# One scaling of the first MLP's weight conversion on GpSimd instead of ScalarE, and no products on constants between the first attention steps

## The chip, the cores and the metric

One core of a Trainium2 chip runs the whole kernel. The metric is device time in microseconds (us) of one execution, as the median of several runs. Engines are called PE (TensorE), DVE (VectorE), ACT (ScalarE), POOL (GpSimd) and SP (SyncE, which issues the DMAs). TensorE's clock has two levels, 1.2 and 2.4 GHz, and the profile gives the granted share of the higher one.

## What is computed

The reference, cut to what matters; everything is float32 outside:

```python
# q, k, v: [4, 8, 576, 64]
scores = q @ k^T / 8 - slope[h] * |i - j|, kept where 0 <= i - j < 128
attn = softmax(scores) @ v                      # -> x: [2304, 512]
h = x @ w_in                                    # w_in: [512, 2048]
x = (h * clip(h + 3, 0, 6) / 6) @ w_out         # w_out: [2048, 512]
xn = x / rms(x) * rms_g
x = (silu(xn @ w_gate) * (xn @ w_val)) @ w_out2 # 512 -> 1536 -> 512
```

The weights reach the chip as 64-bit words, and the kernel turns each into a float32 and splits that into a high and a low part for PE.

## The kernel before

The 2304 tokens are 18 tiles of 128, in six blocks of three tiles. Attention is worked out for a pair of heads and one query tile at a time (class `Step`): `scores` on PE, `bias` on DVE (L366), `exp` on ACT (L381), the reciprocal of the sum on POOL (L383 adds a constant, L384 takes the power -1), `divide` on DVE (L389), `transpose` on PE (L395), `weights` on ACT (L400, a copy out of PSUM), `values` on PE (L413). When a pair of heads has its three tiles, `finish` (L322 on ACT, L323 on DVE) splits the result for the MLP. The parts of one step are spread over consecutive time slots, one or a few in each: scores, bias and exp in one slot, divide in the next, the transpose in the one after it, the values in a fourth.

The order of the work is written out by hand and each engine works through its own queue in that order. There are two parts that matter here.

*Stage A*, in the text below: the loop over `AHEAD` = 15 slots at L568, ahead of the first MLP. In each slot PE gets scores, transposes and values of three different attention steps, and then `busy(1)` (L564), a product of a constant tile with itself whose result nobody reads; PE runs it as two passes. Before the loop there are three more of these (`busy(WARM)`). In slots 4 to 11 the stages of the conversion of the weight units 0 and 1 are mixed in (L590, L591).

*Stage B*: the steps of the first MLP, a loop at L690 over 12 of the 16 chunks of the hidden layer for block 0, and then over all 16 for block 1. One step m does `product1` (L476; 12 products, x by w_in) into one PSUM bank, the attention's transposes, scores and values of this slot, relu on ACT (L714), the product h * min(r, 6) on DVE (L715, one input from PSUM), divide, a copy of the high part on ACT (L720), bias, the low part on DVE (L726), exp, and `product2` of the step before (L489; 9 products by w_out). Until the sixteen weight units are converted, each step also carries one unit (L739 to L744). After that, some 135 us into the span, the kernel goes on with the other blocks and the second MLP. Of the diff, these later parts see only a new argument in a call (L204), with which the instruction stays where it was.

The conversion of one unit, 1024 words in each of 128 partitions, is the generator `convert` (L116). Each `yield` ends one stage, and `First.step(k, stages)` runs the named stages of unit k:

- stage 0: y, the low word scaled (L128, ACT);
- stage 1: x, the high word scaled by 2^-112 (L133, ACT). It reads every other 32-bit word of the raw tile and writes a dense tile, which has two buffers;
- stage 2: the sign bit (L137, DVE);
- stage 3: x and y put together (L140, DVE, two inputs);
- stage 4: the high part for PE (L142, ACT);
- stage 5: the low part for PE (L144, DVE, two inputs).

In a step of stage B, unit k = m + 1 goes through stages 3, 4 and 5, and the unit after it through 0, 1 and 2:

```python
                if k < M1:
                    W1.step(k + 1, 0)
                    W1.step(k, 3, 4)
                    W1.step(k + 1, 1, 2)
                    W1.step(k, 5)
```

So stages 1 of fourteen units stand in stage B, and those of units 0 and 1 in stage A. POOL's queue holds, in a step of stage B with attention, L383 and L384 of that step (its exp stands ahead of the conversion). `load` (L158) brings the raw units by DMAs on SP's queue, some units ahead. The second MLP's weights go through the same generator (L204), with the low word on DVE.

Of the kernel before, what the change touches and what calls it, by code (L numbers as in the profile page):

```python
# [10 lines left out]
F32 = mybir.dt.float32  # L11
# [4 lines left out]
AF = mybir.ActivationFunctionType  # L16
ALU = mybir.AluOpType
# [7 lines left out]
DM = H * D  # L25
# [40 lines left out]
def f32(ap):  # L66
    return ap.bitcast(F32)
# [3 lines left out]
def fused_kernel(ctx: ExitStack, tc: tile.TileContext, qd, kd, v, w1, w2, rms_g, out):  # L71
# [7 lines left out]
    vec, act, pool, pe, sp = nc.vector, nc.scalar, nc.gpsimd, nc.tensor, nc.sync  # L79
# [33 lines left out]
        pool.memset(rel_split[HALF:, : P + HALF], BIG)  # L113


    def convert(raw, n, p, y_bufs, x_bufs, low_on):  # L116

        words = raw.bitcast(U32).rearrange("p (n t) -> p n t", t=2)
        low, high = words[:, :, 0], words[:, :, 1]
        y = p.tile([P, n], U32, tag="wy", name="wy", bufs=y_bufs) if y_bufs else low
        if low_on is act:
            act.activation(y, low, AF.Copy, scale=7.49 * 2.0**-32)  # L128
        else:
            vec.tensor_scalar(y, low, 29, None, ALU.logical_shift_right)  # L130
        yield
        x = p.tile([P, n], F32, tag="wx", name="wx", bufs=x_bufs)
        act.activation(x, high.bitcast(F32), AF.Copy, scale=2.0**-112)  # L133
        yield
        quarters = raw.bitcast(U16).rearrange("p (n t) -> p n t", t=4)
        halves = y.bitcast(U16).rearrange("p (n t) -> p n t", t=2) if y_bufs else quarters[:, :, :2]
        vec.tensor_scalar(halves[:, :, 1], quarters[:, :, 3], 0x8000, None, ALU.bitwise_and)  # L137
        yield
        xi = x.bitcast(U32)
        vec.scalar_tensor_tensor(out=xi, in0=xi, scalar=3, in1=y, op0=ALU.logical_shift_left, op1=ALU.bitwise_or)  # L140
        t = yield x
        act.copy(t[:, 0], x)  # L142
        yield
        vec.tensor_sub(t[:, 1], x, f32(t[:, 0]))  # L144
        yield

    def room(k, shape, dtype, name):
        return wpool.tile(shape, dtype, tag=f"w{k}", name=name)

    class First:  # L150
# [12 lines left out]
        def step(self, k, *stages):  # L163

            for i in stages if k < M1 else ():
                if i == 0:
                    self.runs.append(convert(self.raw[k], 2 * DM, cpool, 2, 2, act))
                if i == 4:
                    t = room(k, [P, 2, 2 * DM], F32R, "w")
                    self.tiles.append(t)  # L170
                    self.runs[k].send(t)
                else:
                    next(self.runs[k])
# [9 lines left out]
    class Second:  # L183
# [17 lines left out]
        def begin(self):  # L201

            if self.raw:
                self.run = convert(self.raw.pop(0), DM, wcpool, 1, 3, vec)  # L204
                for _ in range(3):
                    next(self.run)

# [63 lines left out]
    class Pair:  # L271
# [42 lines left out]
        def finish(self):  # L314

            nq = self.n * P
            x = self.acc.rearrange("p u q -> p (u q)")[:, :nq]
            if self.j == 0:
                xs = (x0pool if self.b == 0 else xpool).tile([P, KC, 2, 3 * P], F32R, tag="xs", name="xs")
                xs_of[self.b] = [xs[:, c] for c in range(KC)]  # L320
            t = xs_of[self.b][self.j]
            act.copy(t[:, 0, :nq], x)  # L322
            vec.tensor_sub(t[:, 1, :nq], x, f32(t[:, 0, :nq]))  # L323

    class Step:
# [12 lines left out]
        def scores(self):  # L338
            pr, c0, k0 = self.pair, self.c0, (self.i - 1 - self.pair.lo) * P
            for x, y in PARTS_OF if pr.parts else ():  # L340
                for a, s in enumerate(self.s):
                    rows = slice(a * D, (a + 1) * D)
                    pe.matmul(  # L343
                        s[:, c0:],
                        lhsT=pr.qs[rows, x, self.u * P : (self.u + 1) * P],
                        rhs=pr.ks[rows, y, k0 + c0 : k0 + 2 * P],
                        start=(x == 0 and y == 0),
                        stop=(x == 1),
                    )
            for a, s in enumerate(self.s if not pr.parts else ()):  # L350
                rows = slice(a * D, (a + 1) * D)
                pe.matmul(  # L352
                    s[:, c0:],
                    lhsT=pr.qr[rows, self.u * P : (self.u + 1) * P],
                    rhs=pr.kr[rows, k0 + c0 : k0 + 2 * P],
                    start=True,
                    stop=True,
                )
# [70 lines left out]
    for k, pr in enumerate(pairs):  # L429
        b, j = divmod(k, H // 2)  # L430
        if b < 2:
            t0, plan = 3 * j if b == 0 else AHEAD - 3 + 3 * j, {"S": (0, 1, 2), "D": (1, 2, 3), "T": (2, 3, 4), "V": (3, 4, 5)}
        else:
            t0, plan = AHEAD + M1 * (b - 1) - 4 + 4 * j, {"S": (0, 0, 2), "D": (1, 1, 3), "T": (None, 3, None), "L": (1, None, 3), "V": (4, 4, 4)}
        slots["Q"].setdefault(t0 - (2 if b < 2 else 1), []).append(pr)
        for u in range(pr.n):
            step = Step(pr, u)
            for kind, at in plan.items():
                if at[u] is not None:
                    slots[kind].setdefault(t0 + at[u], []).append(step)  # L440

    def at(t):
        return [slots[kind].get(t, []) for kind in KINDS]

    def prepare(pairs_, steps):

        for pr in pairs_:
            pr.split() if pr.parts else pr.scale()
        for x in steps:
            k = pairs.index(x.pair) + 2  # L450
            if x.last and k < len(pairs):
                pairs[k].load()
# [98 lines left out]
    cpool = conv.enter_context(tc.tile_pool(name="cpool", bufs=2))  # L551
# [10 lines left out]
    def busy(n):  # L562
        for _ in range(n):
            pe.matmul(warm[:, : 2 * P], lhsT=rel[:, :P], rhs=rel, start=True, stop=True)  # L564
# [3 lines left out]
    for t in range(AHEAD):  # L568
        q, s_, d_, t_, _, v_ = at(t)
        scores(s_, t % 2)  # L570
        for x in t_:
            x.transpose()
        for x in v_:
            x.values()
        busy(1)
        for x in t_:
            x.weights()
        for x in s_:
            x.bias()
        prepare(q, s_)  # L580
        for x in d_:
            x.divide()
        for x in v_:
            if x.last:
                finish(x.pair)
        for x in s_:
            x.exp()
        if t == 2:
            W1.load(3)
        W1.step(0, *{4: (0,), 5: (1, 2), 7: (3,), 9: (4, 5)}.get(t, ()))  # L590
        W1.step(1, *{8: (0,), 11: (1, 2)}.get(t, ()))  # L591
# [83 lines left out]
    for p, (b, m0, m1) in enumerate(PARTS):  # L675
        n = BLOCKS[b][1]
# [13 lines left out]
        for m in range(m0, m1):  # L690
# [3 lines left out]
            if p == 3 and m == 2:  # L694
                first.close()
                wcpool = second.enter_context(tc.tile_pool(name="wcpool", bufs=1, side="right", **OPEN))
# [40 lines left out]
            if p < 2:  # L737
                k = m + 1 if p == 0 else CUT + 1 + m
# [10 lines left out]
            if last:  # L749
# [6 lines left out]
                for x in early:  # L756
                    k = m - EARLY[x.m]
# [20 lines left out]
    n = 3 * P  # L778
# [208 lines left out]
```

## Time and profile before

| what | us |
|---|---|
| median of 3 runs | 967.47 (966.93 to 967.69) |
| the profiled execution | 966.15 |
| its span, first to last instruction | 964.4 |
| PE busy | 948.7 (98%) |
| DVE busy | 640.4 (66%) |
| ACT busy | 454.8 (47%) |
| POOL busy | 183.7 (19%) |

Times in rows are counted from the start of the span. In a row of the timeline the brackets say how long the engine was idle before the instruction and what ended that. A group's row gives the busy time of all, the mean of one in ns, and behind the bar the idle time before them. In the chain of waits each piece is the time from one release to the next, so that pieces add up to the span. A busy PE is not PE at its peak.

### The profile page before, as it was taken

How to read it: one execution, taken by the hardware profiler on the slowest of the kernel's cores; microseconds unless marked ns; L12 is line 12 of the kernel's file. 1: busy time of each engine (PE TensorE's matmuls, PEld its weight loads, DVE VectorE, ACT ScalarE, POOL GpSimd, SP SyncE). 2: the span in 40 equal slices, each digit the busy share in tenths (PEclk: the TensorE clock that was granted, in tenths of full speed). 3: DMA queues.
4: the chain of work that ended last, by engine and by line, in shares of the span. 5: the costliest groups of instructions: out<-in, count | busy, mean ns of one | idle time of the engine just before them, and what ended most of it. 6: DMA issues, size and time to landing. Idle time of an engine off the chain costs nothing.

```text
span 964.4 us, 14723 instructions
## 1 busy us (share of the span) xinstructions
PE 948.7 (98%) x5366; PEld 835.6 (87%) x5366; DVE 640.4 (66%) x1336; ACT 454.8 (47%) x969; POOL 183.7 (19%) x327
## 2 busy tenths in 40 slices
PE   8999999999999999999999999999999999999998
PEld 5687778888888888888999999999999999999996
DVE  5788774454788777777567657787645577545555
ACT  6899763354656655665455453433132323131120
POOL 4333012222322422332033222210000000000000
PEclk9999999999999999999999999999999999999999
DMA  7446511113466465554436757876657555755521
GB/s 230 166 162 196 225 31 31 31 50 107 158 213 200 145 190 169 171 166 135 140 130 226 265 223 278 323 277 232 229 201 275 216 215 217 262 197 205 212 96 65
DMA packets 67432, 175.02 MB, mean 181 GB/s; under 512 B 5024, under 2 KB 41888, under 8 KB 62624
## 3 DMA queue, kind: packets, MB, share of 16 engines
q1 hardware_dynamic: 67360, 174.09, 51.8%
q8 instruction: 42, 0.69, 0.3%
q14 instruction: 30, 0.25, 0.1%
HBM read 130.03 MB, written 44.04 MB: 180 GB/s over the span
## 4 chain that ended last, share of the span: by engine, by line
PE 89%; DVE 5%; ACT 3%; issue 1%; DMA 1%; POOL 0%; ACTq 0%; POOLq 0%; DVEq 0%
PE ps_o L489 19%; PE ps_h L476 19%; PE ps_y L874 15%; PE ps_o L827 10%; PE ps_S L827 8%; PE ps_A L827 6%; PE ps_h L827 4%; PE ps_av L413 3%; PE ps_t L395 2%; PE ps_s L352 2%; PE ps_s L343 1%; ACT wx L133 1%; PE warm L564 1%; DMA wraw<-w 1%; DVE wx L140 1%
## 5 line engine op out<-in xcount | busy, mean ns | idle before, releaser
L489 PE MATMUL ps_o<-w,g 128*128 128x512 f32 x864 | 223.4, 401 | 3.3 <-DVE w L144 3.0
L476 PE MATMUL ps_h<-xs,w 128*128 128x384 f32 x1152 | 223.0, 342 | 0.1
L476 PEld LDWEIGHTS ps_h<-xs,w 128*128 128x128 f32 x1152 | 202.0, 189 | 4.8 <-PE warm L564 0.5
L489 PEld LDWEIGHTS ps_o<-w,g 128*128 128x128 f32 x864 | 157.0, 188 | 43.1 <-DVE w L144 6.2
L874 PE MATMUL ps_y<-wo,g 128*128 128x512 f32 x648 | 150.2, 390 | 0.5 <-DVE g L863 0.5
L874 PEld LDWEIGHTS ps_y<-wo,g 128*128 128x128 f32 x648 | 121.4, 188 | 25.1 <-DVE g L863 0.9
L715 DVE SCALAR_TENSOR_TENSOR t<-t,ps_h 128x384 f32<-128x384 f32 x96 | 53.1, 554 | 120.3 <-ACT t L714 120.2
L714 ACT ACTIVATE t<-ps_h,three 128x384 f32<-128x384 f32 x96 | 55.7, 580 | 99.7 <-PE ps_h L476 99.7
L881 DVE TENSOR_TENSOR y<-y,ps_y 128x512 f32<-128x512 f32 x90 | 61.7, 685 | 35.0 <-PE ps_y L874 34.8
L720 ACT CAST g<-t 128x384 fp32r<-128x384 f32 x96 | 49.3, 513 | 52.2 <-DVE t L715 51.0
L381 ACT ACTIVATE t<-t,m 128x128 f32<-128x128 f32 (+1 forms) x144 | 61.1, 426 | 21.5 <-DVE t L373 10.5
L383 POOL TENSOR_SCALAR r<-den 128x2 f32<-128x2 f32 x72 | 30.1, 418 | 215.1 <-ACT t L381 214.3
L850 ACT ACTIVATE r<-r 128x384 f32<-128x384 f32 x36 | 18.9, 525 | 104.6 <-DVE r L849 104.6
L827 PE MATMUL ps_o<-S,tw 128*128 128x384 f32 x336 | 66.2, 339 | 0.3 <-DVE t L847 0.3
L726 DVE TENSOR_TENSOR g<-t,g 128x384 fp32r<-128x384 f32 x96 | 54.5, 567 | 13.9 <-ACT g L720 12.4
L827 PEld LDWEIGHTS ps_o<-S,tw 128*128 128x128 f32 x336 | 59.3, 188 | 1.4 <-DVE u L838 0.8
L384 POOL TENSOR_TENSOR r<-r,minus 128x2 f32<-128x2 f32 x72 | 55.8, 775 | 6.0
L402 POOL TENSOR_SCALAR_AFFINE_SELECT pt<-pt 128x256 f32<-128x256 f32 x82 | 36.8, 449 | 95.6 <-ACT pt L400 92.7
L835 ACT COPY s<-ps_S 128x384 f32<-128x384 f32 x18 | 8.6, 480 | 89.7 <-PE ps_S L827 89.7
L366 DVE CUSTOM_DVE_ANT_0 t<-ps_s,rel 128x256 f32<-128x256 f32 (+2 forms) x128 | 45.2, 394 | 4.2 <-PE ps_s L352 4.2
L140 DVE SCALAR_TENSOR_TENSOR wx<-wx,wy 128x512 uint32<-128x512 uint32 (+1 forms) x52 | 44.2, 849 | 0.0
L133 ACT ACTIVATE wx<-wraw 128x512 f32<-128x512 f32 (+1 forms) x52 | 42.7, 822 | 0.0
(138 smaller groups left out, 1479.3 us busy)
## 6 DMA issues: line engine op xcount, KB each, us to landing
tw<-t SPq DMA_DIRECT2D x52, 896.0 KB, 6.4
wraw<-w SPq DMA_DIRECT2D x36, 512.0 KB, 4.3
wo<-w SPq DMA_DIRECT2D x18, 1024.0 KB, 5.1
wraw<-w SPq DMA_DIRECT2D x16, 1024.0 KB, 7.9
t<-th SPq DMA_DIRECT2D x12, 896.0 KB, 4.4
t<-tl SPq DMA_DIRECT2D x12, 896.0 KB, 4.2
b<-wx SPq DMA_DIRECT2D x24, 256.0 KB, 2.5
w<-w SPq DMA_DIRECT2D x12, 512.0 KB, 2.9
```

The costliest lines, as they stand in the source:

```text
L133: act.activation(x, high.bitcast(F32), AF.Copy, scale=2.0**-112)
L140: vec.scalar_tensor_tensor(out=xi, in0=xi, scalar=3, in1=y, op0=ALU.logical_shift_left, op1=ALU.bitwise_or)
L381: act.activation(p, p, AF.Exp, bias=self.m[:, a : a + 1], scale=-1.0, accum_out=self.den[:, a : a + 1])
L384: pool.tensor_tensor(self.r, self.r, minus, ALU.pow)
L476: pe.matmul(ps[:, : n * P], lhsT=w[:, a, c * P : (c + 1) * P], rhs=xs[c][:, b, : n * P], start=(k == 0), stop=(k == 3 * KC - 1),)
L489: pe.matmul(o, lhsT=g[:, a, i * P : (i + 1) * P], rhs=w[:, b], start=(m == first and a == 0 and b == 0), stop=(m == last and a == 1),)
L714: act.activation(r[:, :nq], ps[:, :nq], AF.Relu, bias=three)
L715: vec.scalar_tensor_tensor(out=r[:, :nq], in0=r[:, :nq], scalar=6.0, in1=ps[:, :nq], op0=ALU.min, op1=ALU.mult)
L726: vec.tensor_sub(g[:, 1, :nq], r[:, :nq], f32(g[:, 0, :nq]))
L827: pe.matmul(ps, lhsT=w[a][:, k, c * P : (c + 1) * P], rhs=x[:, b, c], start=(start and j == 0), stop=(j == 5), skip_group_check=True,)
L874: pe.matmul(ps, lhsT=gs[i + k][:, a, t // 3, t % 3 * P : (t % 3 + 1) * P], rhs=wo[i + k][:, b], start=(k == 0 and a == 0 and b == 0), stop ...
L881: vec.tensor_add(acc[t], acc[t], ps)
```

## The change

The generator gets an argument that says which engine scales the high word. The first MLP's units pass `pool`, the second MLP's pass `act`, as it was. The product on constants in each of the 15 slots of stage A is left out; the three ahead of the loop stay.

```diff
-    def convert(raw, n, p, y_bufs, x_bufs, low_on):
+    def convert(raw, n, p, y_bufs, x_bufs, low_on, high_on):
...
         x = p.tile([P, n], F32, tag="wx", name="wx", bufs=x_bufs)
-        act.activation(x, high.bitcast(F32), AF.Copy, scale=2.0**-112)
+        if high_on is act:
+            act.activation(x, high.bitcast(F32), AF.Copy, scale=2.0**-112)
+        else:
+            pool.tensor_scalar(x, high.bitcast(F32), 2.0**-112, None, ALU.mult)
         yield
...
-                    self.runs.append(convert(self.raw[k], 2 * DM, cpool, 2, 2, act))
+                    self.runs.append(convert(self.raw[k], 2 * DM, cpool, 2, 2, act, pool))
...
-                self.run = convert(self.raw.pop(0), DM, wcpool, 1, 3, vec)
+                self.run = convert(self.raw.pop(0), DM, wcpool, 1, 3, vec, act)
...
         for x in v_:
             x.values()
-        busy(1)
         for x in t_:
             x.weights()
```

## Rows read from the trace of the kernel before

**Rows 1.** The chain of waits in stage A, one piece: start us, us, what
```profile
20.85 0.63 PE warm L564 x2
```

**Rows 2.** Windows, most of stage A: us, busy per engine, PEclk, DMA share, GB/s
```profile
10.00:40.00 30.00, 27.96 (x199) 16.44 (x200) 22.29 (x86) 24.84 (x73) 12.67 (x27) 1.00 0.51 164
```

**Rows 3.** Waits, 0 to 39 us: us in total, times, longest us
```profile
DVE t L366 <- PE ps_s L352: 4.2, 4, 1.8
...
DVE t L389 <- POOL r L384: 4.0, 9, 0.7
...
DVE w L144 <- ACT w L142: 1.5, 1, 1.5
```

**Rows 4.** The chain of waits in stage B, pieces of product1: start us, us
```profile
62.90 2.12 PE ps_h L476 x12
...
81.82 2.10 PE ps_h L476 x12
...
125.81 3.51 PE ps_h L476 x12
```

**Rows 5.** Groups by shape, 0 to 130 us: busy, mean ns, idle before
```profile
L133 ACT ACTIVATE wx<-wraw 128x1024 f32<-128x1024 f32 x16 | 18.5, 1154 | 0.0
...
L715 DVE SCALAR_TENSOR_TENSOR t<-t,ps_h 128x384 f32<-128x384 f32 x14 | 7.8, 554 | 6.5 <-ACT t L714 6.5
...
L726 DVE TENSOR_TENSOR g<-t,g 128x384 fp32r<-128x384 f32 x14 | 7.7, 553 | 0.7 <-ACT g L720 0.6
```

**Rows 6.** Timeline, steps of stage B: start us, us, instruction, [idle before it]
```profile
42.13 0.55 DVE L715 SCALAR_TENSOR_TENSOR t<-t,ps_h 128x384 f32<-128x384 f32 x1 [2.58 <-ACT t L714]
...
63.69 0.75 POOL L383 TENSOR_SCALAR r<-den 128x2 f32<-128x2 f32 x1 [3.83 <-ACT t L381]
...
64.52 0.95 POOL L384 TENSOR_TENSOR r<-r,minus 128x2 f32<-128x2 f32 x1
...
65.60 1.23 DVE L144 TENSOR_TENSOR w<-wx,w 128x1024 fp32r<-128x1024 f32 x1 [0.17 <-ACT w L142]
...
76.08 1.89 POOL L383 TENSOR_SCALAR r<-den 128x2 f32<-128x2 f32 x1 [3.80 <-ACT t L381]
...
78.06 0.71 POOL L384 TENSOR_TENSOR r<-r,minus 128x2 f32<-128x2 f32 x1
...
78.43 1.23 DVE L144 TENSOR_TENSOR w<-wx,w 128x1024 fp32r<-128x1024 f32 x1 [0.49 <-ACT w L142]
...
79.96 0.55 DVE L715 SCALAR_TENSOR_TENSOR t<-t,ps_h 128x384 f32<-128x384 f32 x1 [0.31 <-ACT t L714]
...
80.43 0.54 DVE L389 TENSOR_SCALAR t<-t,r 128x192 f32<-128x192 f32 x2
```

**Rows 7.** Groups by shape, GpSimd, whole span
```profile
L104 POOL TENSOR_SCALAR_AFFINE_SELECT rel<-rel 128x256 f32<-128x256 f32 x1 | 0.4, 398 | 0.1
...
masks.py:199 POOL TENSOR_SCALAR_AFFINE_SELECT ident<-ident 128x128 f32<-128x128 f32 x1 | 0.3, 293 | 0.1
```

**Rows 8.** Timeline, GpSimd in stage A
```profile
24.67 0.22 POOL L383 TENSOR_SCALAR r<-den 128x2 f32<-128x2 f32 x1 [0.83 <-ACT t L381]
```

**Rows 9.** Waits, 48 to 97 us (stage B, nearly eight steps)
```profile
PEld ps_o L489 <- DVE w L144: 2.9, 6, 0.8
...
DVE t L715 <- ACT t L714: 2.5, 8, 0.3
```

**Rows 10.** Timeline at 494 us: a GpSimd sum and a VectorE instruction
```profile
494.33 0.73 POOL L243 TENSOR_TENSOR tx<-tx 128x256 f32<-128x256 f32 x1
...
494.39 1.08 DVE L726 TENSOR_TENSOR g<-t,g 128x384 fp32r<-128x384 f32 x1 [0.58 <-ACT g L720]
```

**Rows 11.** Windows around a fall of the granted clock (columns as in rows 2)
```profile
122.90:125.20 2.30, 0.02 (x1) 0.05 (x1) 2.02 (x4) 1.68 (x3) 0.00 (x0) 1.00 0.00 0
...
126.00:129.50 3.50, 3.50 (x13) 3.06 (x14) 3.01 (x4) 2.37 (x3) 0.00 (x0) 0.51 0.02 5
```

**Rows 12.** Timeline, PE in stage A
```profile
30.43 0.43 PE L395 MATMUL ps_t<-ident,t 128*128 128x128 f32 x2 [1.27 <-DVE t L389]
```

## The prediction

> **What bounds the kernel now.** I read the page first: the matrix engine (PE) is busy 98% of the span, so only places where it waits, or works on what nobody needs, can give time back. The code that the diff touches runs in the first 135 us alone, and the chain of the work that ended last shows what sets the pace there. The reader is to see two stages.
>
> *Stage A* (5 to 39 us): fifteen attention steps before the first MLP. Nearly every step's piece of the chain holds a product on constants, 0.63 us of PE [rows 1]. It looks as if PE set the pace. The windows of this stage correct that: of 30 us VectorE (DVE) is busy 22.3 and ScalarE (ACT) 24.8 [rows 2]. The waits of the stage say who is late next: DVE waits for PE's scores 4.2 us in four waits, 1.8 of it before the first scores of all; it waits for GpSimd's (POOL's) reciprocal 4.0 us in nine, and 1.5 us once for ACT's cast of a weight unit [rows 3].
>
> *Stage B* (39 to 135 us): each step has a product1, a product2 and one weight unit. A unit goes through wy (L128), L137, wx (L133), L140, L142, L144. Three steps of the chain take 81.82 - 62.90 = 18.92 us, 6.3 a step [rows 4], and pieces of L133 stand on it. ACT spends 18.5 us on its sixteen L133 [rows 5]; that is its busy time, not what its absence is worth. In the timeline of a step, L144 on DVE waits for L142 on ACT, which waits for L140 on DVE. L133 delays none of these three. It delays L714, and DVE's next work, L715, waits 0.31 for it [rows 6]. So L133 costs 0.3 a step: L144 holds DVE until that short before L715.
>
> **Part 1, the products on constants.** Fifteen steps give up 0.63 us each, 9.5 us of PE work. Not more can come back than DVE waits for PE: 4.2 less the first 1.8, so 2.4 us [rows 3]. Not less than nothing, as long as the clock holds (below). I take **-0.8 us**, a third: DVE already waits for the reciprocal in nine steps of fifteen [rows 3], and scores that come earlier turn partly into a longer wait for that, or for ACT's cast.
>
> **Part 2, the new instruction.** POOL does what L133 did: 1024 elements a partition, one input. No such instruction is in the trace. The nearest one-input rows are affine_select, 0.29 us for 128 elements and 0.40 for 256 [rows 7]: 0.82 ns an element, so 0.398 + 768 x 0.00082 = **1.03 us**. For the lower end I put the smallest tensor_scalar, 0.22 us for two elements [rows 8], beside the 0.40 for 256: 0.7 ns an element, 0.93 us. For the upper end the 256-element time is taken four times, 1.59 us. I choose 1.03, as the two rows that differ in nothing but length are nearest.
>
> *In stage A* two are moved. ACT is freed of two, POOL's queue gets two, and the next reciprocal (L383, L384), for which DVE's L389 waits, queues behind each. If nothing hides that, it costs 2 x 1.03 = 2.1 us; if POOL has room and ACT was last at one of them, one L133 is gained, 18.5 / 16 = 1.1 us [rows 5]. Neither end is nearer to a row, so I take the middle, **+0.5 us**.
>
> *In stage B* fourteen are moved. The gain: L715's waits for L714 sum to 6.5 us in fourteen [rows 5], of which the first, 2.58 at 42.13, is the start of the stage [rows 6]. The other thirteen, 3.9 us, vanish: **-3.9 us**. PE can follow: in the stretch where these waits are gone in eight steps (2.4 us), PE waits 2.9 us for L144 [rows 9].
>
> The price: POOL and DVE keep each other out. POOL's 128x2 L383 needs 0.22 us alone [rows 8] but 1.89 while L140 and L137 run on DVE [rows 6]. It holds the other way too: L726, 0.55 us in the mean [rows 5], takes 1.08 when it starts 0.06 after a POOL sum of 0.73 [rows 10]. DVE was free to start when POOL had run 0.59 us, 0.14 before its end. So a POOL wx of 1.03 us keeps such a DVE instruction out for 0.89 us. With PSUM as one input DVE is not kept out: L383 takes 0.22 in the middle of L323 [rows 8].
>
> Now place it. On POOL it stands behind L383 and L384 of its step, both of which are themselves late. In the step at 76 us L384 ends at 78.77, L144 has begun at 78.43, so POOL begins when that ends, 79.66. L715 reads PSUM and runs at once. L389, due 0.47 after it, at 80.13, is held until 79.66 + 0.89 = 80.55, that is 0.42 late [rows 6]. Five of the nine steps with attention are like this one (L383 of 1.08 or 1.89 us). In the other four (L383 of 0.75, as at 63.69) L384 ends at 65.47 and POOL's next begins some 0.08 later, 0.05 before L144 at 65.60 [rows 6]. If POOL is first, L144 is 0.84 late, and with it product2 on PE; if L144 is first, L389 is 0.42 late again. That is too near to call, so I take the middle, 0.63. Sum: 5 x 0.42 + 4 x 0.63 = **+4.6 us** (ends 3.8 and 5.5). In the five steps without scores ahead POOL has nothing else, runs beneath L715 and the wait for L720's cast, and costs nothing; without that cover it would be 0.4 each. No DMA is issued or moved. POOL's queue is free again some 1.7 us before the next L383.
>
> The Trainium skill ("SBUF — State Buffer", section "SBUF: two separate sides") says that whichever of the two starts first has the shared pair for the whole instruction. The trace agrees that it is a hold and no sharing, but shows DVE starting 0.14 us before POOL's end; by the rule the nine steps would cost 9 x 0.14 = 1.3 us more, and the sum below would be +1.7.
>
> **Sum:** -0.8 + 0.5 - 3.9 + 4.6 = **+0.4 us** on the profiled execution's 966.15 us (span 964.4 us). The median of the runs shown is 967.47, 1.3 above it, so the forecast is 967.47 + 0.4 = **967.9 us**: no change that can be measured. A measurement of this kernel can tell about 0.2% (1.9 us) from none.
>
> **The rivals.** *Slower: POOL's instruction is long.* At 1.59 us each hold is 0.56 longer; place: L389 or L144 in nine steps, 9 x 0.56 = 5.0 us, so +5.4 and **972.9**. It decides from about 1.2 us on, where the sum passes 0.2%. For it: a two-input sum of 256 elements takes POOL 0.73 us [rows 10], so POOL is slow where it has more to do, and the input has every other word. Against it: the two one-input rows. The Trainium skill ("GPSIMD Engine Reference", section "Performance pitfalls for Q7 kernels") gives about 1.9 cycles an element for steps of up to 8 bytes; an estimate from that page is 1024 x 1.9 / 1.2 GHz = 1.6 us, and no row here shows such a step on POOL.
>
> *Faster: the hold costs nothing.* If POOL's instruction finds gaps of DVE (it waits 0.49 us for L142 and 0.31 for L714 in the step at 76 us [rows 6]) or lets DVE pass, the 4.6 falls away: -4.2, **963.3**. Against it speaks L726's 1.08; for it, that no row shows a POOL instruction as long as this one beside DVE.
>
> *The clock.* At 122.9 to 125.2 PE was idle 2.3 us, and from 126.0 to 129.5 the granted clock was 0.51, that is 1.2 instead of 2.4 GHz; product1 took 3.5 us there instead of 2.1 [rows 4, 11]. In stage A PE waits 1.27 us before 30.43 [rows 12], and the clock stays at 1.00 [rows 2]; without the 0.63 us product before that wait the gap grows to 1.9 [rows 1, 12]. If the clock falls there too, +1.4 us: **969.3**. The Trainium skill ("TensorE: Matmul & The Clock Gate", section "Part 1") says that activity is what releases the throttle, so that products on constants do work by being there; by that page stage A could lose more than once.
>
> **How the numbers follow.** Forecast 0.40, long POOL instruction 0.26, no hold 0.20, clock 0.14. The forecast's own bounds (parts 1 and 2 at their ends, -2 and +3) put 0.04 of it below and 0.02 above the 0.2%; of the clock's case 0.06 stay within. Faster: 0.20 + 0.04 = 0.24. Within: 0.34 + 0.06 = 0.40. Slower: 0.26 + 0.02 + 0.08 = 0.36. The range reaches from the case without a hold to that of the long instruction, 963.4 to 973.2; the forecast's own is 966 to 970.
>
> **What would show it.** Right: POOL's wx near 1.03 us; L715's waits for L714 gone; in their place L389 about 0.4 late behind POOL, L144 late in some steps; three steps of the chain at 18.9 to 19.3 us; a stage A shorter by half a microsecond or so; PE in stage A waiting more, at a clock of 1.00. Wrong: a wx of 1.5 us or more; no wait of L389 or L144 for POOL; a granted clock of 0.5 before 39 us; a chain that loses or gains time after 135 us, where nothing was changed.

## The result, and the profile after

The changed kernel took **974.11 us** (median of 6 runs) against 967.42 for the kernel before, run beside it: 1.0072 times as long, 95% interval [1.0061, 1.0083], so 7.0 us slower by the ratio. The forecast was 967.9 with a range up to 973.2; the result lies just above the range. Two later comparisons gave 1.0068 [1.0052, 1.0083] and 1.0058 [1.0044, 1.0071].

The page's group of the moved instruction, and the groups of VectorE in stage B (39 to 144 us), after; the columns are those of [rows 5]:

```profile
L136 POOL TENSOR_SCALAR wx<-wraw 128x1024 f32<-128x1024 f32 x16 | 52.1, 3261 | 4.1 <-DVE w L147 4.1
...
L143 DVE SCALAR_TENSOR_TENSOR wx<-wx,wy 128x1024 uint32<-128x1024 uint32 x15 | 19.1, 1276 | 1.7 <-POOL wx L136 1.7
...
L717 DVE SCALAR_TENSOR_TENSOR t<-t,ps_h 128x384 f32<-128x384 f32 x16 | 8.8, 547 | 3.6 <-ACT t L716 3.6
```

wx takes 3.26 us in the mean where the forecast had 1.03. (From L133 on, line numbers after are three higher, behind the loop of stage A two higher.) The waits of L717 (the old L715) for the relu are gone except one: 3.6 us, all of it in one wait.

Windows after, columns as in [rows 2]: four of stage A and the start of stage B, then one in the middle of stage B.

```profile
10.00:20.00 10.00, 9.28 (x56) 5.36 (x54) 6.02 (x27) 7.63 (x25) 3.51 (x8) 0.67 0.82 303
20.00:30.00 10.00, 6.41 (x44) 3.98 (x45) 7.32 (x23) 6.73 (x22) 7.19 (x10) 0.85 0.23 70
30.00:40.00 10.00, 6.82 (x58) 4.12 (x56) 8.66 (x27) 6.61 (x20) 5.70 (x7) 0.98 0.23 72
40.00:50.00 10.00, 8.65 (x46) 7.20 (x45) 4.08 (x18) 4.45 (x14) 3.02 (x7) 0.66 0.66 245
60.00:70.00 10.00, 9.93 (x59) 7.85 (x60) 9.24 (x22) 7.06 (x18) 9.77 (x5) 1.00 0.80 272
```

Two things have changed. The granted clock, 1.00 in all of stage A before [rows 2], falls three times before 50 us. And GpSimd, busy some 40% of stage A, is busy 9.77 of 10 us in the middle of stage B.

Where the time went, by the starts of TensorE's product1 in both traces: the first starts at 43.54 instead of 39.12 (+4.4 us); the third at 56.74 instead of 49.93 (+6.8); the fifteenth at 134.15 instead of 125.56 (+8.6). From 144 us on the distance is constant, +7.7; the 0.9 between is made up where the clock fell before, at 126 us [rows 11], and did not fall after. So more than half is lost in stage A, where the forecast had -0.3, and 2.4 of the rest in the first two steps of stage B.

Here is the place in stage A where the first wx runs, timeline after: start us, us, instruction, [idle before it]; then two rows of the same place in the kernel before.

```profile
19.50 0.71 POOL L387 TENSOR_TENSOR r<-r,minus 128x2 f32<-128x2 f32 x1
...
20.18 2.83 POOL L136 TENSOR_SCALAR wx<-wraw 128x1024 f32<-128x1024 f32 x1
20.25 1.43 DVE L392 TENSOR_SCALAR t<-t,r 128x256 f32<-128x256 f32 x2 [0.48 <-POOL r L387]
...
21.56 0.63 PE L398 MATMUL ps_t<-ident,t 128*128 128x128 f32 x4 [1.73 <-DVE t L392]
...
22.29 0.94 DVE L302 TENSOR_SCALAR qraw<-qraw,qscale 128x384 f32<-128x384 f32 x1
...
23.10 0.23 POOL L386 TENSOR_SCALAR r<-den 128x2 f32<-128x2 f32 x1
...
24.16 0.48 DVE L392 TENSOR_SCALAR t<-t,r 128x128 f32<-128x128 f32 x2 [0.93 <-POOL r L387]
```

```profile
19.06 0.62 DVE L389 TENSOR_SCALAR t<-t,r 128x256 f32<-128x256 f32 x2 [0.47 <-POOL r L384]
...
21.36 0.48 DVE L389 TENSOR_SCALAR t<-t,r 128x128 f32<-128x128 f32 x2
```

When the reciprocal (L387) ends, it releases two things at once: wx, next in GpSimd's queue, and VectorE's L392, which waits for that reciprocal. wx is first by 0.07 us, and L392's pair takes 1.43 us instead of 0.62. TensorE waits 1.73 us for it. That is one delay, the hold. The other is the queue: the next reciprocal (L386 at 23.10) begins when wx has ended, and the next L392 waits 0.93 us for it. That L392 comes 3.91 us after the one before it, against 2.30 in the kernel before.

The chain of waits says which delay counts here: it does not go through the held pair but through wx and the reciprocal behind it (start us, us, what):

```profile
20.21 2.81 POOL wx L136
...
23.10 0.23 POOL r L386
...
23.40 0.73 POOL r L387
...
24.16 0.30 DVE t L392
```

It does so again at the second wx, from 37.02, at both in wx_only and after_third below, and at the first in wx_only_again. In after_again it goes through the held pairs instead, and through TensorE at its lower clock behind them. So the hold is not far behind the queue.

Of the 4.4 us, 1.2 are lost before the first wx starts (20.25 against 19.06), and 3.2 from there to the first product1 (23.29 us against 20.06).

In stage B the chain of waits after runs through GpSimd (start us, us, what):

```profile
63.77 1.79 POOL r L386
...
65.64 0.72 POOL r L387
66.36 3.58 POOL wx L136
...
69.97 1.24 DVE wx L143
```

wx, then the two halves of the reciprocal behind it: 3.6 + 1.8 + 0.7 = 6.1 us of a step of 6.4. GpSimd is at its limit there. Yet the step is hardly longer: from the fifth to the eighth product1 three steps take 88.44 - 69.22 = 19.2 us after, 18.9 before [rows 4]. What stage B loses beyond its first two steps is 1.8 us up to the fifteenth product1, in a few single steps.

### The profile page after: what moved, and what is told of

Its sections match the earlier page's. It is cut to its first block, busy times and chain, and to the rows that moved or that the text cites. A ratio compares the mean times of both kernels' runs of the same rounds, so it can differ in the third digit from the quotient of the medians.

```text
span 972.3 us, 14661 instructions
## 1 busy us (share of the span) xinstructions
PE 946.0 (97%) x5336; PEld 834.7 (86%) x5336; DVE 649.3 (67%) x1336; ACT 439.1 (45%) x953; POOL 242.2 (25%) x343
## 4 chain that ended last, share of the span: by engine, by line
PE 85%; DVE 5%; POOL 5%; ACT 3%; issue 2%; ACTq 0%; POOLq 0%; DVEq 0%
PE ps_o L492 18%; PE ps_h L479 18%; PE ps_y L876 15%; PE ps_o L829 10%; PE ps_S L829 8%; PE ps_A L829 6%; PE ps_h L829 4%; PE ps_av L416 3%; POOL wx L136 3%; PE ps_t L398 2%; PE ps_s L346 1%; POOL r L386 1%; PE ps_s L355 1%; DVE w L147 1%; POOL r L387 1%
## 5 line engine op out<-in xcount | busy, mean ns | idle before, releaser
L717 DVE SCALAR_TENSOR_TENSOR t<-t,ps_h 128x384 f32<-128x384 f32 x96 | 53.1, 553 | 116.5 <-ACT t L716 116.4
L386 POOL TENSOR_SCALAR r<-den 128x2 f32<-128x2 f32 x72 | 33.1, 460 | 163.8 <-ACT t L384 162.2
L852 ACT ACTIVATE r<-r 128x384 f32<-128x384 f32 x36 | 18.9, 526 | 106.9 <-DVE r L851 106.9
L387 POOL TENSOR_TENSOR r<-r,minus 128x2 f32<-128x2 f32 x72 | 56.2, 780 | 6.0
L136 POOL TENSOR_SCALAR wx<-wraw 128x1024 f32<-128x1024 f32 x16 | 52.1, 3261 | 4.1 <-DVE w L147 4.1
L398 PE MATMUL ps_t<-ident,t 128*128 128x128 f32 x190 | 35.7, 291 | 14.4 <-DVE t L392 12.6
```

The costliest lines, as they stand in the source:

```text
L136: pool.tensor_scalar(x, high.bitcast(F32), 2.0**-112, None, ALU.mult)
L387: pool.tensor_tensor(self.r, self.r, minus, ALU.pow)
L398: pe.transpose(self.ps[:, a, c], self.t[:, a, c * P : (c + 1) * P], ident)
L717: vec.scalar_tensor_tensor(out=r[:, :nq], in0=r[:, :nq], scalar=6.0, in1=ps[:, :nq], op0=ALU.min, op1=ALU.mult)
```

## The experiments

Two theories to begin with. *POOL*: the long wx is the loss, as a hold on VectorE and as GpSimd's queue. *Clock*: without the products the granted clock falls in stage A. One more kernel, forms, was executed once (974.9 us), for its trace. All ratios are against the kernel before, run beside each on the same chip, whose median was 966.6 to 966.9; 0.1% is 1 us. "First product1" is its start in the trace, 39.12 before and 43.54 after.

| kernel | wx | products | ratio [95%] | first product1 |
|---|---|---|---|---|
| products_only | ScalarE | out | 0.9996 [0.9987, 1.0006] | 38.52 |
| wx_only | GpSimd | kept | 1.0054 [1.0041, 1.0068] | 42.30 |
| half_first | half on GpSimd, stage B | kept | 0.9984 [0.9975, 0.9993] | 38.78 |
| after_again | GpSimd | out | 1.0068 [1.0052, 1.0083] | 42.00 |
| late_units | GpSimd in stage B only | out | 1.0021 [1.0012, 1.0030] | 38.76 |
| pool_copy | GpSimd, a copy | out | 1.0030 [1.0014, 1.0047] | 41.64 |
| copy_later | the same, later in stage A | out | 1.0016 [1.0006, 1.0025] | 40.78 |
| no_wx | none | kept | 0.9972 [0.9960, 0.9984] | 38.99 |
| no_wx_no_products | none | out | 0.9953 [0.9937, 0.9970] | 39.80 |
| wx_only_again | GpSimd | kept | 1.0044 [1.0029, 1.0059] | 44.82 |
| after_third | GpSimd | out | 1.0058 [1.0044, 1.0071] | 42.73 |

### One part of the change at a time

products_only, against before:

```diff
-        busy(1)
```

> Only the products on constants are left out; ScalarE scales the high words as before. Theory 'clock' (the fall of TensorE's granted clock in stage A comes from the missing products alone and is most of the loss): granted clock 0.5 in records before 48 us, first product1 at 41 to 43.5 us instead of 39.12, program 1.5 to 4.5 us slower than before. Theory 'POOL' (the 2.83 us instruction is the loss): granted clock 1.00 in stage A, first product1 at 38.3 to 39.2, program 0 to 0.8 us faster. Theory 'both together' (the clock falls only where wx lengthens TensorE's gaps too): clock 1.00 or one short fall, within 1 us of before.

Measured: 0.9996, first product1 0.60 us earlier, still 0.61 earlier at 144 us. Windows of this kernel, columns as in [rows 2]:

```profile
10.00:20.00 10.00, 8.34 (x57) 5.02 (x58) 6.69 (x30) 8.36 (x26) 3.70 (x8) 0.83 0.81 293
20.00:30.00 10.00, 6.49 (x57) 3.80 (x55) 7.40 (x28) 8.04 (x24) 4.57 (x8) 1.00 0.31 92
30.00:40.00 10.00, 9.05 (x62) 6.04 (x63) 7.61 (x31) 8.40 (x26) 4.03 (x9) 0.83 0.30 95
```

The clock does fall, in two of three windows, and it costs nothing that shows: TensorE has room here (6.49 of 10 us busy where the clock is full). So neither theory had it whole. The missing products are enough for a fall; this fall is not the loss. What TensorE did before a fall is seen best in the changed kernel, windows of after, and then the first stretch in the kernel before:

```profile
21.00:27.40 6.40, 3.81 (x33) 2.68 (x34) 5.47 (x18) 3.61 (x12) 5.02 (x6) 0.96 0.30 93
27.50:30.90 3.40, 3.40 (x21) 1.91 (x21) 1.34 (x7) 3.21 (x8) 1.75 (x4) 0.58 0.06 15
```

```profile
21.00:27.40 6.40, 6.14 (x44) 3.40 (x44) 4.71 (x17) 5.59 (x17) 3.34 (x7) 1.00 0.35 104
```

Busy 3.81 of 6.40 us, then a clock of 0.58; before, with the products, 6.14 of 6.40 and no fall. The Trainium skill ("TensorE: Matmul & The Clock Gate", section "Part 1") says that activity is what releases the throttle, and the traces agree so far that the clock fell where TensorE had done less.

wx_only, against after:

```diff
+        busy(1)
```

> Only wx goes to GpSimd; the products on constants stay. Theory 'POOL': each wx 2.8 us in stage A and 3.6 in stage B; two of them delay stage A by 1.5 to 2.5 us (first product1 at 40.6 to 41.6); GpSimd paces the steps with scores (wx 3.6, r 1.8 and 0.7: 6.2 to 6.4 us a step), clock 1.00 before 48 us, program 3 to 5 us slower than before. Theory 'clock': first product1 before 40.3, program 0 to 1.5 us slower than before. Theory 'both together': 1.5 to 3.5 us slower, clock 1.00.

Measured: 1.0054, +5.2 us. First product1 42.30 (+3.2), at 144 us +4.7. Timeline of wx_only in stage A:

```profile
18.87 2.85 POOL L136 TENSOR_SCALAR wx<-wraw 128x1024 f32<-128x1024 f32 x1
18.93 1.45 DVE L392 TENSOR_SCALAR t<-t,r 128x256 f32<-128x256 f32 x2 [0.48 <-POOL r L387]
```

The same collision with the products kept, at a granted clock of 1.00 from 10 to 30 us. Here too the chain goes through wx and the reciprocal behind it, for 2.82 us at 18.90 and 2.83 at 35.72. That is the POOL theory, and stage A is dearer than even it had (40.6 to 41.6).

### What wx costs on GpSimd, and why

forms: the sixteen wx in four shapes in turn.

```diff
+            form = len(W1.runs) % 4 if W1.tiles else 0
...
+                    pool.tensor_scalar(x[:, c], high.bitcast(F32)[:, c], 2.0**-112, None, ALU.mult)
...
+                pool.tensor_copy(x, high.bitcast(F32))
+                pool.tensor_scalar(x, x, 2.0**-112, None, ALU.mult)
```

> As wx_only, but the sixteen wx take turns in four forms: one instruction of 1024 (as in after), four of 256, a copy of 1024 from every other word followed by a product by a number in place on dense words, two of 512. If the every-other-word input is what makes it slow: the dense product takes 0.9 to 1.6 us and the copy 2.8. If the operation is slow whatever the layout: both 2.8, 256 columns 0.7 and 512 columns 1.4. If a fixed part is large: 256 columns take over 0.9.

Timeline of forms, GpSimd in stage A, where little runs beside it:

```profile
20.23 2.85 POOL L138 TENSOR_SCALAR wx<-wraw 128x1024 f32<-128x1024 f32 x1
...
37.01 1.12 POOL L144 COPY wx<-wraw 128x1024 f32<-128x1024 f32 x1
38.21 2.79 POOL L145 TENSOR_SCALAR wx<-wx 128x1024 f32<-128x1024 f32 x1
```

It is the operation. The copy from every other word takes 1.12 us, the product on dense words 2.79, as much as on every other word. The 512-column form takes 1.54 where VectorE does not hinder it, so 2.85 - 1.54 = 1.31 us for 512 columns more: 2.6 ns an element and a fixed part of 0.2. (Four of 256 took 3.98, all of them beside VectorE's work.) The Trainium skill ("GPSIMD Engine Reference", section "Performance pitfalls for Q7 kernels") prices a read by its step, some 1.9 cycles at steps up to 8 bytes, by which an estimate was 1.6 us. That a step of 8 bytes costs no more than dense words agrees with it; that the operation changes the time 2.5 times is not in it, and the estimate fits neither.

This allows the sharpest test of the forecast: a wx of the size that it assumed. In pool_copy wx is that copy. The exponent is mended by an exclusive-or in the two VectorE instructions that follow in any case, so nothing is added.

```diff
-            pool.tensor_scalar(x, high.bitcast(F32), 2.0**-112, None, ALU.mult)
+            pool.tensor_copy(x, high.bitcast(F32))
...
+            vec.tensor_scalar(halves[:, :, 1], quarters[:, :, 3], 0x8000, 0xC000, ALU.bitwise_and, ALU.bitwise_xor)
...
+        vec.scalar_tensor_tensor(out=xi, in0=xi, scalar=3, in1=y, op0=ALU.logical_shift_left, op1=ALU.bitwise_or if high_on is act else ALU.bitwise_xor)
```

> After, with wx as a copy on GpSimd (the exponent is mended by an exclusive-or in the two VectorE instructions that follow, so nothing else is added): 1.1 us alone instead of 2.83. If the size of that one instruction was the step that failed: the forecast's sum with 1.1 for 1.03, +0.5 to +1.5 us, 967.1 to 968.1; VectorE's relu wait gone, reciprocals 0.4 late. If GpSimd's hold is not the price at this size: 3 to 4.5 us faster than before. If the clock falls in stage A even so: 1.5 to 4 us slower than before.

Measured: 1.0030, +2.9 us, against +6.6 for the changed kernel beside it. So the length of wx is worth 3.7 us (by the medians, 970.53 and 972.97, 2.4), and 2.9 us stay although wx has the forecast's size. They are not in stage B alone (the 0.5 to 1.5 us expected from the size alone are missed; the 1.5 to 4 us expected if the clock falls in stage A even so are met, and it does fall). The first product1 is at 41.64, nearly as late as in after_again (42.00). Timeline of pool_copy in stage A:

```profile
19.04 1.09 POOL L136 COPY wx<-wraw 128x1024 f32<-128x1024 f32 x1
19.13 1.43 DVE L395 TENSOR_SCALAR t<-t,r 128x256 f32<-128x256 f32 x2 [0.48 <-POOL r L390]
```

L395 (the L392 of this kernel) takes 1.43 us behind a GpSimd instruction of 1.09 just as behind one of 2.83. **The hold of a VectorE instruction that starts just behind it is 0.81 us in both, and does not grow with the length.** The Trainium skill ("SBUF — State Buffer", section "SBUF: two separate sides") lets whoever starts first have the shared pair for the whole instruction; beside the copy that fits within 0.2 us, beside the 2.83 us product it does not: VectorE gets in some 2 us before its end. A later part of the long instruction keeps out other work, though: L302 takes 0.94 at 22.29 after, 0.42 in the mean before the first MLP in products_only.

With the short copy the queue is no longer in the way: the next L395, at 21.64, waits for nothing, nor does the one at 38.48 behind the second copy. What costs time is the held pair and, behind it, TensorE's clock. Windows of pool_copy, the first with TensorE's wait of 1.73 us for that pair, the second behind it:

```profile
18.00:20.40 2.40, 0.71 (x6) 0.30 (x4) 1.92 (x7) 1.33 (x5) 2.17 (x4) 1.00 0.23 72
21.00:24.00 3.00, 3.00 (x17) 1.69 (x18) 2.87 (x9) 1.59 (x6) 1.70 (x3) 0.50 0.03 5
```

From the L395 at 19.13 the next comes only 0.2 us later than in the kernel before (2.51 us against 2.30), but the third one 1.6 us later (8.23 against 6.65). The chain between goes through TensorE at half clock, from 21.07 to 24.74.

### Is it the hold, the queue or the clock in stage A?

copy_later, against pool_copy: in stage A the copy waits until VectorE has begun its products with the reciprocal, by a one-column memset of its tile behind them.

```diff
+        W1.step(0, *{6: (2,)}.get(t, ()))
+        W1.step(1, *{12: (2,)}.get(t, ()))
...
+                vec.memset(x[:, :1], 0.0)
             pool.tensor_copy(x, high.bitcast(F32))
```

> As the kernel with wx as a copy on GpSimd, but in stage A the copy is made to wait until VectorE has begun its next product with the reciprocal (a one-column memset of the tile behind that product, on VectorE), one step later than before. Theory 'the hold' (wx starts on GpSimd at the moment at which its own reciprocal releases VectorE's product, and keeps that product out for 0.85 us, twice): the two products take 0.62 instead of 1.43, first product1 at 39.0 to 40.3 instead of 41.64, program 1 to 2.5 us faster than with the copy at its old place (968 to 969.5). Rival 'the queue' (the next reciprocal waits for wx, wherever it stands): first product1 at 41 to 42.2, no gain. Rival 'the clock': the products are short but records of 0.5 stay between 20 and 48 us, first product1 at 40.5 to 41.6.

Timeline of copy_later:

```profile
20.26 0.62 DVE L401 TENSOR_SCALAR t<-t,r 128x256 f32<-128x256 f32 x2 [0.48 <-POOL r L396]
...
20.97 1.14 POOL L143 COPY wx<-wraw 128x1024 f32<-128x1024 f32 x1 [0.74 <-DVE wx L142]
...
21.49 0.83 DVE L311 TENSOR_SCALAR qraw<-qraw,qscale 128x384 f32<-128x384 f32 x1
22.19 0.22 POOL L395 TENSOR_SCALAR r<-den 128x2 f32<-128x2 f32 x1
```

The two products with the reciprocal are back at 0.62 us, and the first product1 comes at 40.78, 0.86 us earlier than with the copy in its old place; 1.0016 against 1.0030, medians 968.60 and 970.53 (the intervals overlap). The next reciprocal (L395) still stands behind the copy, and VectorE's product with it now waits 0.92 us; the gain came in spite of that queue. It is at the low end, and the first product1 is later than the 40.3 expected: the hold has moved to L311 (0.83 instead of 0.42), and in this profile the clock had fallen before the first copy ran (0.66 from 10 to 20 us). From 20 us on it is 1.00, as it was not in pool_copy (0.83 and 0.90 in the next two windows). The first product that pool_copy holds starts 1.13 us later here, at 20.26, so from there on copy_later takes 20.52 us to its first product1 and pool_copy 22.51. These 2.0 us are the hold and the falls of the clock behind it together: both are absent in copy_later from 20 us on, so it does not tell one from the other. By its number alone, 40.78 would also lie in the rival's range (40.5 to 41.6), whose falls between 20 and 48 us are not there.

late_units, against after:

```diff
-                    self.runs.append(convert(self.raw[k], 2 * DM, cpool, 2, 2, act, pool))
+                    self.runs.append(convert(self.raw[k], 2 * DM, cpool, 2, 2, act, act if k < 2 else pool))
```

> After, with the first two units' wx back on ScalarE; the other fourteen stay on GpSimd, the products stay out. Theory 'stage A is most of it' (two wx of 2.83 us ahead of the reciprocal, and the clock that falls with them): first product1 at 38.3 to 38.8, no record of 0.5 after 41 us, stage B costs 1 to 2 us, program 0.3 to 1.5 us slower than before. Rival 'stage B is most of it' (GpSimd as the pace): 3.5 to 5.5 us slower than before although stage A is as fast as without the products.

Measured: 1.0021, first product1 38.76. Beside after_again's 1.0068 in the same comparison: the first two units, of sixteen, cost 0.47%, **4.5 of 6.6 us**; the other fourteen 2.0, or 2.4 over products_only. The theory that stage A is most of it is right, though its 0.3 to 1.5 us for the rest was too little.

### Are the products worth keeping once wx is on GpSimd?

after_again, after_third (the changed kernel unaltered) and wx_only_again:

> The changed kernel unaltered, beside the others of this group. From its first profile: granted clock 0.5 in records between 10 and 48 us, first product1 near 43.5, the constant part after 144 us +7.7. If the falls of the clock in stage A belong to this kernel, they are here again and it is 1 to 3 us slower than the kernel that moved wx and kept the products (+5.1 us); if they were chance, this profile has a clock of 1.00 and the loss is 5 to 5.5 us.

> wx on GpSimd, products kept, once more, beside the changed kernel on the same chip: what the products are worth when wx is there. If they keep the clock up for the delayed stage A: 1.2 to 3 us less than the changed kernel. If they only cost their time: 0 to 0.6 us more than it.

> The changed kernel beside the one that keeps the products: 1.2 to 3 us slower than that if the falls of the clock in stage A are a price, and its profile shows between three and six records of 0.5 before 48 us; equal or 0.6 faster if not.

The clock falls in stage A in every profile of the changed kernel. It also falls in the profiles that keep the products with wx on GpSimd, once each in stage A and later: wx_only 0.83, wx_only_again 0.73, forms 0.83 from 30 to 40 us. Windows of after_again:

```profile
10.00:20.00 10.00, 8.03 (x54) 4.75 (x54) 6.47 (x28) 7.80 (x26) 4.32 (x9) 0.83 0.79 291
20.00:30.00 10.00, 8.22 (x58) 4.91 (x58) 6.98 (x24) 6.89 (x19) 6.87 (x9) 0.83 0.23 68
30.00:40.00 10.00, 6.88 (x40) 4.24 (x42) 8.48 (x27) 5.98 (x20) 5.69 (x7) 0.71 0.23 72
```

The price as a whole stays open. Within one comparison the changed kernel is 1.0058 and the one that keeps the products 1.0044: 1.4 us apart, but the intervals overlap. Single profiles show why it is hard to tell: where a fall lies differs from one to the next. In the first profile of after, one covers the first product1 (3.89 us for eleven of its products from 43.54; twelve take 2.36 before), and the third product1 is 2.4 us further behind than the first. In after_again no fall lies there, and it is 0.6 further behind. (wx_only_again's first product1 of 44.82 is such a single profile too.)

One part of it can be read. All eight profiles without the products have a fall that begins some 10 us in, before any wx runs on GpSimd. In three (after, copy_later, no_wx_no_products) it is longer, 0.66 or 0.67 in the window from 10 to 20 us, and VectorE's product that stands at 19.06 before starts at 20.25 to 20.30. In four of the other five the window has 0.83, in products_only among them, and the product starts at 18.93 to 19.15; in after_again, also at 0.83, at 19.44. no_wx_no_products, against products_only further up:

```profile
10.00:20.00 10.00, 9.32 (x56) 5.38 (x54) 6.01 (x27) 7.58 (x24) 3.44 (x8) 0.66 0.79 288
```

So the longer early fall goes with a loss of 0.8 to 1.4 us; the 1.2 us that the changed kernel's first profile lost before its first wx are of this kind.

### What the old place on ScalarE was worth

no_wx takes wx away altogether: L146 reads the high words where they lie. The products stay, so the diff is against wx_only; the exclusive-or is that of pool_copy.

```diff
-            pool.tensor_scalar(x, high.bitcast(F32), 2.0**-112, None, ALU.mult)
+            pass
...
+        vec.scalar_tensor_tensor(out=xi, in0=xi if high_on is act else high, scalar=3, in1=y, op0=ALU.logical_shift_left, op1=ALU.bitwise_or if high_on is act else ALU.bitwise_xor)
```

> Before with wx left out altogether: the instruction that joins the words reads the high words where they lie and mends the exponent by an exclusive-or; the products stay. If ScalarE's wx was worth L715's waits for the relu: 3 to 4.5 us faster than before (963.7 to 962.2), L715 waits under 0.5 us in all for L714 after the first step. If something else ends next (scores, VectorE): 0 to 1.5 us faster. If reading every other word makes the joining instruction longer than 1.22 us: that, times fourteen, back.

Measured: 0.9972, -2.7 us; 3.1 earlier at 144 us. VectorE in stage B, no_wx:

```profile
L146 DVE SCALAR_TENSOR_TENSOR wx<-wraw,wy 128x1024 uint32<-128x1024 uint32 x15 | 18.3, 1217 | 0.0
...
L721 DVE SCALAR_TENSOR_TENSOR t<-t,ps_h 128x384 f32<-128x384 f32 x17 | 9.3, 547 | 4.9 <-ACT t L720 4.9
```

Reading every other word costs the joining instruction nothing (1217 ns; 1219 before), and no wait for the relu is left among the waits from 48 to 97 us. That is less than the 3 to 4.5 us expected: the waits went, and the time gained is 2.7 us, not the 3.9 that they summed to. In the trace 2.05 us are gained in stage B up to the fifteenth product1 (123.38 against 125.56, less the 0.13 of stage A); another 0.9 come right behind it, where the clock fell before [rows 11] and does not fall here.

half_first, against before, tries to have part of it: GpSimd scales 512 columns, first in its queue in the step.

```diff
+        if early:
+            x = p.tile([P, n], F32, tag="wx", name="wx", bufs=x_bufs)
+            pool.tensor_scalar(x[:, :early], high.bitcast(F32)[:, :early], 2.0**-112, None, ALU.mult)
+            yield
```

> Before, with the last fourteen units' wx cut in two: GpSimd scales the first 512 columns, first in its queue in the step, ScalarE the other 512 where it stood; products kept, units 0 and 1 on ScalarE. If ScalarE's wx is what makes L715 late and GpSimd has room once its instruction is short and stands ahead of the reciprocal: L715's waits for the relu (3.9 us in thirteen) go, program 2 to 3.9 us faster. If GpSimd's hold on VectorE is the price whatever its place: each step gives back 0.4 or more, program 0 to 2 us slower. Duration of the half: 1.4 us if it goes by the element (2.83 / 2), more if much of 2.83 is fixed.

Measured: 0.9984, -1.5 us, between the two. Timeline of half_first, GpSimd:

```profile
63.94 1.55 POOL L128 TENSOR_SCALAR wx<-wraw 128x512 f32<-128x512 f32 x1 [5.68 <-DMA wraw<-w]
65.57 0.59 POOL L395 TENSOR_SCALAR r<-den 128x2 f32<-128x2 f32 x1
```

The half is short enough, but first in the queue it waits for its unit's DMA in some steps, and the reciprocal stands behind it.

no_wx_no_products is no_wx with the changed kernel's other edit.

> Both kernels' costs left out: no wx on any engine, no products on constants in stage A. If the products' absence is worth what it was alone (-0.6): 962.5 to 963.5, 0.35 to 0.45% faster than before. If VectorE's hold is what made their absence harmful, the clock may fall in single records of stage A without a loss; if the clock alone did, first product1 comes at 39.5 or later and the gain of the kernel without wx shrinks to 0.1 to 0.2%.

Measured: **0.9953 [0.9937, 0.9970], 961.94 us**, faster than both kernels. That is 1.8 us less than no_wx, in another comparison (the intervals overlap a little). The profiled executions do not show these 1.8 us: 963.29 and 963.39, and 3.0 and 3.1 us earlier than before at 144 us. The clock is 0.66 from 10 to 20 and from 30 to 40 us, and the first product1 is at 39.80, later than in no_wx (38.99) and by the sign that was named for a cost of the clock (39.5 or later). What the products are worth without wx is therefore not shown either.

## Why the prediction was wrong

*Part 1, the products, -0.8.* The size came out: -0.6 by the trace of products_only. The condition did not: the text put it at no loss "as long as the clock holds", and the clock fell twice in that very profile. With the longer early fall the same stage is 0.7 us later than before (no_wx_no_products, 39.80). So the number owes something to luck.

*Part 2, wx of 1.03 us, 1.59 at most.* **This is the step that failed most.** It measured 2.83. The two rows "that differ in nothing but length" [rows 7] were of another operation. A copy does cost 1.1 by that slope; a product with a number does not. The size is worth 2.4 to 3.7 us (pool_copy against after_again).

*Part 2 in stage A, +0.5.* The second step that failed, in part through the first. The text put +2.1 for the next reciprocal queued behind each wx, -1.1 for ScalarE set free, and took the middle because "neither end is nearer to a row". wx_only gives +3.2 (42.30 - 39.12), above the upper end. The queue was the right question: the chain in wx_only and after goes through wx and the reciprocal behind it, twice. With 2.83 us the upper end would have been 2 x 2.83 = 5.7; 3.2 of that showed. What the text lacked is the hold in this stage. It had nearly the right price, 0.89 us against 0.81, and spent it in stage B only. It did not ask what is released together with wx: the L389 whose reciprocal has just ended. wx stands right behind that reciprocal in the queue, so the two start together each time. With a wx of the forecast's size this is what is left: pool_copy's first product1 is 2.5 us late, with no wait in the queue behind either wx, over the held pair and the fall of the clock behind it. How these two share the 2.5 us stays open.

*Part 2 in stage B, -3.9 and +4.6.* Both terms were too large, and their sum came out near by luck. Up to the fifteenth product1 no_wx gains 2.05 us in stage B. A wx of the forecast's size costs there 1.55 us in pool_copy (4.07 - 2.52) and 0.75 in copy_later (2.41 - 1.66). So its price is 2.8 to 3.6, where the forecast's own way with 1.1 us gives 5.2 (4.6 + 9 x 0.07). The long wx makes stage B 2.4 us dearer than products_only (late_units). L392 is 0.4 us late in these steps, as forecast (0.93 instead of 0.54 at 67.60 after), with an instruction nearly three times as long.

*The rivals.* "POOL's instruction is long" gave 972.9, near the result, but by the wrong mechanism: its holds were to grow with the length, in nine steps of stage B, and they did not grow; the cost is in stage A and in GpSimd's queue. "The clock falls in stage A" came true, at a price that is known in part only. "No hold" is refuted by each trace with wx on GpSimd. Of the signs that the text listed, three steps of the chain at 18.9 to 19.3 us and L715's waits gone were seen, as were those for wrong: a wx above 1.5 us and a granted clock of 0.5 before 39 us.

*The range.* Its upper end is the rival with a wx of 1.59 us in stage B. A wx of 2.83 us, and a stage A beyond its upper end of +2.1, were in none of its cases.

## What to carry to other kernels

When an instruction is moved to another engine's queue, ask two things. What stands behind it there, and who waits for that? And what does the instruction ahead of it release? That work and the moved instruction start together, and if they keep each other out they collide every time. Price it by a row of the same operation, not only of the same shape. And before moving an instruction off a busy engine, see whether its neighbours can absorb it: here leaving it out was worth 2.7 us, and moving it alone cost 4 to 5.

## What the runs showed of the hardware

GpSimd's product of 1024 float32 elements a partition by a number takes 2.8 us, dense or from every other word, where VectorE does not hinder it; its copy takes 1.1. A VectorE product by a number between SBUF tiles that starts 0.07 to 0.09 us behind such an instruction is kept out for 0.8 us, whether that lasts 1.1 or 2.8 us. And the granted clock fell to its lower level in stage A in all eight profiles without the products on constants, and later in the stage in the three that kept them with wx on GpSimd. In products_only the falls cost nothing that shows; the longer early fall went with 0.8 to 1.4 us.
